# Units 2 and 3 move to the split convolution, with new instruction orders for the first eight tiles

## The chip, the core and the metric

The kernel runs on one core of one Trainium2 chip. The metric is the device time of one execution in microseconds (us): the median of three runs before the change is 705.1 us, with 704.99 and 705.26 as the lowest and the highest. The profile is of a fourth execution of its own; it took 705.18 us, of which the profiler's span, from the first to the last instruction that it shows, is 703.5 us. The remaining 1.7 us lie around the span.

## What is computed

A causal convolution of seven taps over the sequence, with one softmax-normalised set of taps for each of eight heads, followed by a two-layer feed-forward block whose activation is h·cos(h):

```python
def _attn_ref(x, weight):                 # x: 8 x 4096 x 192, weight: 8 x 7
    w = weight - np.max(weight, axis=-1, keepdims=True)
    w = np.exp(w)
    w = w / (np.sum(w, axis=-1, keepdims=True) + 1e-09)
    x_pad = np.concatenate([np.zeros((B, pad, D), dtype=np.float32), x], axis=1)
    idx = np.arange(S)[:, None] + np.arange(K)[None, :]
    x_unf = x_pad[:, idx, :].reshape(B, S, K, H, group)
    return np.einsum('hk,bskhg->bshg', w, x_unf).reshape(B, S, D)

def _moe_ref(x, w_in, w_out):             # 32768 tokens, 192 -> 2048 -> 192
    h = x @ w_in
    g = h * np.cos(h)
    return (g @ w_out).astype(np.float32)
```

## The kernel before

**Units and tiles.** The 32768 tokens are cut into 32 *units* of 1024 tokens. A unit is convolved and turned (transposed) so that the channels lie on partitions; then its two *tiles* of 512 tokens run through the feed-forward block. There are 64 tiles, called t0 to t63 below.

**A tile.** `mm1` (line 503) makes one of eight pairs of rows of `h` in PSUM with six matmuls; it is written `h0` to `h7` in the orders. `gcu` (lines 510 and 514) makes the cosine on ScalarE (ACT) and the product `g` on VectorE (DVE); this is `s0` to `s7`. `mm2_step` (line 552) is one step of the second product, two matmuls that sit in the two halves of the array's rows; `m13` is thirteen steps. A tile has 64 steps, and the steps of a tile lag its `h` by most of a tile. `h` has three PSUM buffers (`h_pool`, line 73), each of two banks, which the convolution of the next units also takes. The two output banks are copied out by `P` (ACT) and `Q` (DVE), line 571, and stored by `O`, line 574.

**Two ways to convolve.** Units 0 to 3 (`FIRST_RAW = 4`) are *whole*: `cast_unit` (`K`, line 219, GpSimd, here POOL) makes bf16; `conv_part` (line 229) runs four matmuls of 216 columns over all 128 rows for each of two halves of the heads, `d` and `c`; ACT copies them out (`ed`, `ec`, line 239); `double_unit` (`D`, line 307, POOL) doubles the result; `turn_unit` (`X`, line 326) turns 27 blocks by one DMA transpose; `mend_edges` (`Y`, line 394, POOL) repairs the first tokens of each block. Units 4 on are *split*: of a unit's nine blocks, five of 112 tokens go to TensorE in `conv_unit` (`c1`, `c2`, line 277: two groups of eight matmuls that use the two halves of the rows), ACT copies them out (line 294), and two transposes of 15 blocks turn them (`X` and `x`, line 317). The other 464 tokens are turned first (`T`, `turn_raw`, line 345), three taps are multiplied on ACT (`a`, line 356, six instructions a unit), the other four taps and all sums run on POOL (`R`, `conv_raw`, lines 363 to 377), and four DMAs put the result in place (`U`, `spread_raw`, line 387).

**What sets the order.** There is no scheduler: the program is recorded as it is written out in `PE_ORDER`, `ACT_ORDER`, `PE_FIRST` and `ACT_FIRST`, one string for each tile, and each engine runs its own instructions in that order. A letter in a PE string stands for matmuls (`h`, `m`, `c`, `d`, `r`, `w`) or for work of POOL or of SyncE (SP) that is recorded at that place: `K+3` in tile t is the cast of unit t//2+3, `L` its load, `T+3` its raw turn. `PE_FIRST` and `ACT_FIRST` hold the tiles with orders of their own, of which the last two of PE already resemble the later ones.

**The turn.** Where matmuls of the two row halves change places on one bank, `Turn` puts a no-operation on SP: it waits for the last matmul before the change (`mark`), and the first matmul after it waits for the no-operation (`wait`). That happens once a tile (between steps 31 and 32, lines 555 to 559) and once in each `conv_unit` (between `c1` and `c2`, lines 285 and 290). SP is also the queue from which nearly all loads, turns and stores are issued, in the order in which they were recorded. So TensorE can go on past these two points only when SP has got through everything recorded before.

```python
        turn = Turn()
        turn.mark(*ms)          # SP waits for the end of c1
        yield
        for h in range(4):
            ms = mm(h + 4, 0), mm(h, 1)
            if h == 0:
                turn.wait(*ms)  # c2 waits for SP
```

Of the kernel before, what the change touches and what calls it, by code (L numbers as in the profile page):

```python
# [16 lines left out]
def kernel(  # L17
# [8 lines left out]
    nc = tc.nc  # L26
    B, S, D = x.shape
    H, K = weight.shape
# [3 lines left out]
    T = 512  # L32
    NT = NTOK // T
    NB = T // 128
    U = 1024
    NU = NTOK // U
    UB = U // 128
    UPS = S // U
    TPU = U // T
    NF = Dff // 128  # L40
    NP = NF // 2
    NC = D // 64
    R = G // NC

    FIRST_RAW = 4
    NPB, OP = 5, 112
    NRB = 4
    OR = (U - NPB * OP) // NRB  # L50
# [1 line left out]
    PA = 3  # L52
# [120 lines left out]
    ct_bufs = [consts.tile([128, 2 * NC * NPB + 1, 64], BF16, name="ct_buf%d" % i) for i in range(2)]  # L173
# [166 lines left out]
    rT, pa, ro = {}, {}, {}  # L340
# [11 lines left out]
    def taps(u, j, half, mul):  # L352
        if u not in pa:
            pa[u] = pa_pool.tile([128, PA, WN, OR], FP32, name="pa")
        part = slice(HALF * half, HALF * (half + 1))
        mul(pa[u][:, j, part], tap_window(u, j)[:, part], tap[:, j : j + 1])  # L356

# [1 line left out]

    def conv_raw(u):  # L360

        a, p = pa.pop(u), raw_prod
        nc.gpsimd.tensor_tensor(out=p, in0=tap_window(u, PA, K),  # L363
                                in1=tap[:, PA:K].rearrange("p (j a b) -> p j a b", a=1, b=1).to_broadcast([128, K - PA, WN, OR]),
                                op=ALU.mult)
        add = nc.gpsimd.tensor_tensor
        n, done = K - PA, 0
        while done < PA:
            m = min(n, PA - done)
            add(out=p[:, 0:m], in0=p[:, 0:m], in1=a[:, done : done + m], op=ALU.add)  # L370
            done += m
        while n > 2:
            m = n // 2
            add(out=p[:, 0:m], in0=p[:, 0:m], in1=p[:, n - m : n], op=ALU.add)  # L374
            n -= m
        ro[u] = ro_pool.tile([128, WN, OR], BF16, name="ro")
        add(out=ro[u], in0=p[:, 0], in1=p[:, 1], op=ALU.add)  # L377
# [35 lines left out]
    for i, k in enumerate("DPDPDPDPDPDPDPAA"):  # L413
        q, rows = divmod(i, 4)
        three[k](out=band[32 * rows : 32 * rows + 32, HQ * q : HQ * (q + 1), 32 * rows : 32 * rows + E],  # L415
                     in_=diag[32 * q : 32 * q + 32])
    cast_unit(0, NB, UB)
    nc.gpsimd.memset(pick, 0.0)
    for i in range(2):
# [157 lines left out]
    def finish(t):  # L577
        o_sb[t] = opool.tile([128, NB, D], FP32, name="o_sb")
        for si in range(2):
            for b in range(2):  # L580
                copies[b](o_sb[t][:, 2 * b + si, :], o_ps.pop((t, b, si)))
                store(t, 2 * b + si, 2 * b + si + 1, [nc.scalar, nc.sync][b])
# [3 lines left out]

    PE_ORDER = ['m12 h0 m4 h1 K+3 R+1 m5 h2 m7 q h3 U+0 m6 h4 m17 h5 X+1 m9 p h6 h7 O m4', 'm11 h0 m4 h1 m6 h2 m7 q x+1 h3 m5 h4 m7 c1 m8 c2 m3 h5 T+3 L+4 m9 p O h6 h7 m4']
    ACT_ORDER = ['s0 s1 a211 s2 s3 s4 a014 a114 Q s5 P s6 s7 a007', 's0 s1 s2 a102 s3 a203 s4 Q ec2 ec1 s5 P s6 s7']  # L590

    PE_FIRST = ["K1 h0a h0b W0 h1 h2 h3 r h4 w5 d11 w4 h5 d21 W1 c11 X0 m1 h6 m11 h7 L2 c21 D1",
                "m6 K2 h0 m1 L3 h1 K3 m13 q h2 m3 h3 m9 h4 m6 h5 m3 X1 c12 m11 p c22 h6 d12 h7 L4 L5 m17 c13 m4 c23 m1 d22 Y1 D2 m1",
                "h0 m2 h1 m7 q K4 h2 m11 h3 X2 O m8 h4 Y2 m13 p h5 h6 m9 h7 m7",
                "h0 m8 h1 m8 q h2 m7 h3 m7 O m1 h4 m3 d13 m4 d23 m6 h5 m4 p T4 h6 h7 m4 D3 Z0 Z1",
                'm12 h0 m4 h1 K+3 m5 h2 m7 q h3 m6 h4 m17 h5 X+1 m9 p h6 h7 O m4',
                'm11 h0 m4 h1 m6 h2 m7 q x+1 Y3 h3 m5 h4 m7 c1 m8 c2 m3 h5 T+3 L+4 m9 p O h6 h7 m4']
    ACT_FIRST = ["s0a s0b s1 s2 er s3 s4 ed11 ed21 s5 ec11 s6 ec21 s7",
                "s0 s1 s2 s3 s4 s5 ec12 ec22 Q P s6 ed12 s7 ed22 ec13 ec23",
                "s0 s1 s2 s3 Q s4 P s5 s6 s7",  # L600
                "s0 s1 s2 s3 s4 ed13 ed23 Q s5 P s6 s7"] + ACT_ORDER

    PE_LAST = "m10 h0 m3 h1 m13 h2 m2 q h3 m10 h4 m3 h5 m7 h6 m12 p h7 O m7"
    ACT_LAST = "s0 s1 s2 s3 s4 s5 s6 P A s7"

    HALVES = {"": (0, NB), "a": (0, NB // 2), "b": (NB // 2, NB), "l": (0, NB // 2), "r": (NB // 2, NB)}
    conv = {"r": conv_rest()}
    for v in (1, 2, 3):
        for i, part in enumerate("dc"):
            conv[part, v] = conv_part(v, i, ring_banks)  # L610
    step, made, stored, done = 0, -1, 0, set()
    for t in range(NT + 1):
        u, second = divmod(t, TPU)
        cu = u + TPU
        if t >= 2 * TPU:
            if second:
                conv["c"] = conv_unit(cu, ring_banks) if cu < NU else iter(())
        pe = PE_LAST if t == NT - 1 else "m%d p" % (2 * STEPS * NT - step) if t == NT else PE_ORDER[second] if t >= len(PE_FIRST) else PE_FIRST[t]
        act = ACT_LAST if t == NT - 1 else ACT_ORDER[second] if t >= len(ACT_FIRST) else ACT_FIRST[t]
        act, h = act.split(), {}  # L620
        done = {k for k in done if k[0] in "cd" and k[2:]}

        def part_of(k):
            return k if k in conv else (k[0], int(k[2])) if k[2:] else k[0]

        def flush():
            while act:
                k = act[0]
                if k[0] == "e":
                    need = k[1:] if k[1:] in conv else k[1] + "2" + k[3:]  # L630
                else:
                    need = "p" if k in "PQA" else "h" + k[3:] if k[0] in "ab" else "h" + (k[1:2] if k[2:] in "lr" else k[1:])
                if need not in done:
                    return
                act.pop(0)
                if k in "PQA":
                    if 0 <= made < NT - 1:
                        evac(made, int(k != "P"), nc.scalar.copy if k == "A" else None)
                elif k[0] in "ab":
                    if u + 2 in rT:  # L640
                        taps(u + 2, int(k[1]), int(k[2]), nc.scalar.mul if k[0] == "a" else nc.vector.tensor_scalar_mul)
                elif k[0] == "e":
                    next(conv[part_of(k[1:])], None)
                elif k[0] == "s" and t < NT:
                    gcu(t, int(k[1]), h[k[1:2] if k[2:] in "lr" else k[1:]], *HALVES[k[2:]])

        def of_unit(k, v):
            if (k, v) == ("K", 1):
                cast_unit(1, 0, NB)
                cast_unit(1, NB)  # L650
            elif k == "Z":
                nc.gpsimd.memset(ct_bufs[v][0:OP], 0.0)
            elif (k, v) == ("X", 0):
                turn_unit(0, NB, UB)
            elif k == "L":
                load_unit(v)
                if v < FIRST_RAW:
                    load_edges(v)
            else:
                {"K": cast_unit, "D": double_unit, "X": turn_unit, "Y": mend_edges, "T": turn_raw, "R": conv_raw,  # L660
                 "U": spread_raw, "x": lambda u: turn_unit(u, part=1)}[k](v)

        for k in pe.split():
            if k[0] == "h":
                if t < NT:
                    h[k[1:]] = mm1(t, int(k[1]), *HALVES[k[2:]])
            elif k[0] in "rdc":
                next(conv[part_of(k)], None)
            elif k[0] == "m":
                for q in range(step, step + int(k[1:])):  # L670
                    mm2_step(q)
                step += int(k[1:])
            elif k[0] == "w":
                keep_warm(int(k[1:]), o_pools[0].tile([128, T], FP32, name="o_ps0"))
            elif k == "p":
                assert step % (2 * STEPS) == 0
                made = step // (2 * STEPS) - 1
            elif k == "q":
                assert step % (2 * STEPS) == STEPS
            elif k[0] == "W":  # L680
                cast_wo(int(k[1]))
            elif k == "O":
                while stored <= made and (stored, 0) in evacs and (stored, 1) in evacs:
                    store(stored)
                    stored += 1
            elif k[1:] and k[1] != "+":
                of_unit(k[0], int(k[1]))
            else:
                if u + int(k[2:]) < NU and (k[0] not in "RUx" or u + int(k[2:]) >= FIRST_RAW):
                    of_unit(k[0], u + int(k[2:]))  # L690
            done.add(k)
            flush()
            if k == "p" and made == NT - 1:
                finish(NT - 1)
        assert t == NT or not act


# [28 lines left out]
```

## Time and profile before

| | |
|---|---|
| median of three runs | 705.1 us |
| profiled execution | 705.18 us, span 703.5 us |
| TensorE (PE), busy | 697.0 us of the span |
| DVE, ACT, POOL, busy | 642.4, 644.4 and 503.7 us |
| granted TensorE clock, mean | 0.999 |
| one pair of tiles later on (from `h0` of t6 at 77.73 us to `h0` of t8 at 99.07 us) | 21.34 us |

The profile is a page of views of one execution. Its timeline names, for each engine, when a run of equal instructions began, how long it took, and what it waited for; the line number is that of the kernel before. "SPq" is the queue of SP: its duration is the time in which SP issues a transfer and can do nothing else, not the time until the data has landed. A mean duration of a matmul contains its latency, and its successors begin earlier: what matmuls cost on a full TensorE is read from the starts of the groups.

### The profile page before, as it was taken

What the parts mean: (1) busy time and instruction counts of PE and PEld (TensorE: products, weight loads), DVE (VectorE), ACT (ScalarE), POOL (GpSimd) and SP (SyncE); (2) the same over time, 40 slices, a digit from 0 to 9 for tenths busy, and PEclk for the clock granted to TensorE, in tenths of its full rate; (3) what the DMA queues carried; (4) which work ended last, traced back from release to release, by engine and by line L of the source; (5) the groups of instructions that cost most, each with busy time, mean ns of one, the idle gap of its engine ahead of it and who ended that gap; (6) DMA issues with size and microseconds to landing.
All of it is one profiled execution on the core that took longest, in us unless ns stands there. A gap on an engine that the chain in (4) does not pass through costs nothing.

```text
span 703.5 us, 26826 instructions
## 1 busy us (share of the span) xinstructions
PE 697.0 (99%) x11830; PEld 512.8 (73%) x11830; DVE 642.4 (91%) x598; ACT 644.4 (92%) x831; POOL 503.7 (72%) x214
## 2 busy tenths in 40 slices
PE   8999999999999999999999999999999999999997
PEld 4677777777777777777777777777777777777776
DVE  6889999999999999999999999999999999999996
ACT  7889999999999999999999999999999999999875
POOL 6524478977778877778877688877789778799400
PEclk9999999999999999999999999999999999999999
DMA  8964456667667768676656577577665576874331
GB/s 214 234 167 97 120 135 143 138 147 164 138 153 146 131 145 176 134 152 131 147 152 153 150 159 129 140 161 150 143 147 132 145 174 137 153 127 95 92 91 47
DMA packets 228292, 100.09 MB, mean 142 GB/s; under 512 B 156240, under 2 KB 227792, under 8 KB 228176
## 3 DMA queue, kind: packets, MB, share of 16 engines
q1 hardware_dynamic: 227464, 97.40, 62.7%
q8 instruction: 92, 1.51, 0.9%
q0 software_dynamic: 416, 0.79, 0.7%
q14 instruction: 24, 0.20, 0.1%
q10 hardware_dynamic: 296, 0.20, 0.1%
HBM read 31.36 MB, written 25.17 MB: 80 GB/s over the span
## 4 chain that ended last, share of the span: by engine, by line
PE 96%; DMA 1%; DVE 1%; POOL 0%; SPq 0%; ACT 0%; issue 0%; POOLq 0%
PE o_ps L552 48%; PE h L503 46%; PE h L277 2%; DMA wo_f<-in_moe_w_out_dram 1%; PE h L552 0%; SPq L124 0%; PE h L229 0%; DVE band L415 0%; POOL wo L120 0%; POOL mask L159 0%; DVE ct L438 0%; PE o_ps L432 0%; ACT mask L164 0%; DVE diag L404 0%; DVE prod L401 0%
## 5 line engine op out<-in xcount | busy, mean ns | idle before, releaser
L514 DVE TENSOR_TENSOR g<-h,cs 128x1024 bf16<-128x1024 f32 (+1 forms) x513 | 604.9, 1216 | 27.9 <-ACT cs L510 24.5
L510 ACT ACTIVATE cs<-h 128x1024 bf16<-128x1024 f32 (+1 forms) x513 | 511.0, 1021 | 44.0 <-PE h L503 30.6
L552 PEld LDWEIGHTS <-g 64*128 64x128 bf16 x8192 | 354.2, 94 | 102.2 <-issue 1.0
L552 PE MATMUL o_ps<-wo,g 64*128 64x192 bf16 x8128 | 420.6, 243 | 0.1
L503 PE MATMUL h<-cT,w 64*128 64x512 bf16 (+1 forms) x3078 | 407.0, 376 | 0.8 <-DVE g L514 0.4
L503 PEld LDWEIGHTS <-w 64*128 64x128 bf16 x3078 | 147.6, 94 | 75.0 <-issue 1.8
L211 POOL CAST xk<-x_f 128x768 bf16<-128x768 f32 (+1 forms) x56 | 76.4, 1367 | 113.9 <-DMA x_f<-in_x_dram 109.3
L363 POOL TENSOR_TENSOR raw_prod<-rT,tap 128x2784 f32<-128x2784 bf16 x28 | 135.3, 4832 | 0.2
L370 POOL TENSOR_TENSOR raw_prod<-raw_prod,pa 128x2088 f32<-128x2088 f32 x28 | 129.1, 4609 | 2.2
L356 ACT ACTIVATE pa<-rT,tap 128x348 f32<-128x348 bf16 x168 | 94.6, 580 | 0.0
L374 POOL TENSOR_TENSOR raw_prod<-raw_prod 128x1392 f32<-128x1392 f32 x28 | 87.9, 3138 | 2.2
L571 DVE COPY o_sb<-o_ps 128x384 f32<-128x384 f32 x62 | 34.6, 557 | 23.7 <-PE o_ps L552 23.5
L377 POOL TENSOR_TENSOR ro<-raw_prod 128x696 bf16<-128x696 f32 x28 | 46.5, 1660 | 2.2
L294 ACT CAST ct_buf<-h 112x480 bf16<-112x480 f32 x56 | 28.6, 562 | 4.1 <-PE h L277 0.6
L571 ACT COPY o_sb<-o_ps 128x384 f32<-128x384 f32 x64 | 30.8, 482 | 0.1
L277 PE MATMUL h<-xk,band 64*112 64x120 bf16 x448 | 21.2, 213 | 0.0
L277 PEld LDWEIGHTS <-band 64*112 64x112 bf16 x448 | 18.0, 127 | 0.0
L219 POOL CAST x_bf<-x_f 128x768 bf16<-128x768 f32 (+2 forms) x5 | 9.1, 1812 | 7.0 <-DMA x_f<-in_x_dram 6.9
L307 POOL COPY ct<-ct 128x1728 bf16<-128x1728 bf16 x3 | 4.9, 1630 | 8.9 <-ACT ct L239 8.9
L394 POOL COPY cT<-cT 128x144 bf16<-128x144 bf16 x3 | 0.9, 308 | 13.5 <-DMA cT<-ct 13.5
L136 PE MATMUL o_ps<-zero 128*128 128x512 bf16 x21 | 7.2, 492 | 1.3 <-DVE zero L131 1.3
L239 ACT CAST ct<-h 128x432 bf16<-128x432 f32 x12 | 5.9, 530 | 0.4 <-issue 0.4
(66 smaller groups left out, 52.7 us busy)
## 6 DMA issues: line engine op xcount, KB each, us to landing
out_dram<-o_sb SPq DMA_DIRECT2D x63, 384.0 KB, 3.7
x_f<-in_x_dram SPq DMA_DIRECT2D x28, 480.0 KB, 5.5
x_f<-in_x_dram SPq DMA_DIRECT2D x56, 192.0 KB, 2.7
cT<-ro SPq DMA_DIRECT2D x112, 87.0 KB, 2.3
x_f<-in_x_dram SPq DMA_DIRECT2D x4, 384.0 KB, 5.6
wo_f<-in_moe_w_out_dram SPq DMA_DIRECT2D x4, 384.0 KB, 7.9
x_f<-in_x_dram SPq DMA_DIRECT2D x2, 768.0 KB, 5.2
cT<-ct_buf SPq DMA_TRANSPOSE x56, 4.0
```

The lines of the kernel that those rows point to most:

```text
L211: copy(out=xk[u][:, NC * n0 : NC * n1].rearrange("p (k n) m -> p k n m", k=NC), in_=x_tiles[u][:, n0:n1].rearrange("p n (m k) -> p k n m", ...
L277: return nc.tensor.matmul(out=ps[h // 4][0:OP, 0 : NPB * 4 * G].rearrange("p (m i r) -> p i m r", m=NC * NPB, i=4)[:, h % 4], lhsT=band[si ...
L356: mul(pa[u][:, j, part], tap_window(u, j)[:, part], tap[:, j : j + 1])
L363: nc.gpsimd.tensor_tensor(out=p, in0=tap_window(u, PA, K), in1=tap[:, PA:K].rearrange("p (j a b) -> p j a b", a=1, b=1).to_broadcast([128, ...
L370: add(out=p[:, 0:m], in0=p[:, 0:m], in1=a[:, done : done + m], op=ALU.add)
L374: add(out=p[:, 0:m], in0=p[:, 0:m], in1=p[:, n - m : n], op=ALU.add)
L377: add(out=ro[u], in0=p[:, 0], in1=p[:, 1], op=ALU.add)
L503: nc.tensor.matmul(out=h[:, i, n0 * 128 : n1 * 128], lhsT=w[rows, k, j, :], rhs=rhs, start=(k == 0), stop=(k == NC - 1))
L510: nc.scalar.activation(out=cs[:, :, part], in_=h[:, :, part], func=AF.Sin, bias=math.pi / 2.0, scale=1.0)
L514: nc.vector.tensor_tensor(out=g_tiles[t][:, 2 * j : 2 * j + 2, part], in0=h[:, :, part], in1=cs[:, :, part], op=ALU.mult)
L552: ms.append(nc.tensor.matmul(out=o_ps[tt, b, si], lhsT=g_tiles[tt][rows, f, s * 128 : (s + 1) * 128], rhs=wo[rows, f // 2, f % 2, :], star ...
L571: (copy or copies[b])(o_sb[t][:, 2 * b : 2 * b + 2, :].rearrange("p s d -> p (s d)"), o_ps.pop((t, b)))
```

## The change

`FIRST_RAW` becomes 2: units 2 and 3 are split too. Their whole path goes (`d12 c12 d13 c13` and their copies, `D2 D3`, `Y2 Y3`, the two DMA transposes of 27 blocks, `load_edges`), and `c1 c2`, `T`, `R`, `U`, `x` and the taps come in. The two buffers `ct_buf` are no longer cleared whole between tiles (`Z0 Z1`, t3); only their unused columns are, at the start, on POOL ahead of the cast of unit 0's second half. Eight tiles instead of six have an order of their own; in t0 the casts and the matmuls keep their order, but three steps and four steps move ahead of `c11` and `h6`, and `c21` is recorded earlier. An `a` may now name its unit in a fourth digit. The marks `p` and `q` go: `m` counts the steps itself.

```diff
-    FIRST_RAW = 4
+    FIRST_RAW = 2
...
+    for buf in ct_bufs:
+        nc.gpsimd.memset(buf[0:OP, 0], 0.0)
+        nc.gpsimd.memset(buf[0:OP, 1:].rearrange("p (k n) m -> p k n m", k=NC)[:, :, NPB:], 0.0)
     cast_unit(0, NB, UB)
...
-    PE_FIRST = ["K1 h0a h0b W0 h1 h2 h3 r h4 w5 d11 w4 h5 d21 W1 c11 X0 m1 h6 m11 h7 L2 c21 D1",
-                "m6 K2 h0 m1 L3 h1 K3 m13 q h2 m3 h3 m9 h4 m6 h5 m3 X1 c12 m11 p c22 h6 d12 h7 L4 L5 m17 c13 m4 c23 m1 d22 Y1 D2 m1",
-                "h0 m2 h1 m7 q K4 h2 m11 h3 X2 O m8 h4 Y2 m13 p h5 h6 m9 h7 m7",
-                "h0 m8 h1 m8 q h2 m7 h3 m7 O m1 h4 m3 d13 m4 d23 m6 h5 m4 p T4 h6 h7 m4 D3 Z0 Z1",
-                'm12 h0 m4 h1 K+3 m5 h2 m7 q h3 m6 h4 m17 h5 X+1 m9 p h6 h7 O m4',
-                'm11 h0 m4 h1 m6 h2 m7 q x+1 Y3 h3 m5 h4 m7 c1 m8 c2 m3 h5 T+3 L+4 m9 p O h6 h7 m4']
-    ACT_FIRST = ["s0a s0b s1 s2 er s3 s4 ed11 ed21 s5 ec11 s6 ec21 s7",
-                "s0 s1 s2 s3 s4 s5 ec12 ec22 Q P s6 ed12 s7 ed22 ec13 ec23",
-                "s0 s1 s2 s3 Q s4 P s5 s6 s7",
-                "s0 s1 s2 s3 s4 ed13 ed23 Q s5 P s6 s7"] + ACT_ORDER
+    PE_FIRST = ["K1 h0a h0b h1 h2 W0 h3 r h4 W1 w5 d21 d11 w4 h5 m3 c11 m4 h6 c21 m4 X0 h7 m1 D1",
+                "L2 m7 h0 h1 L3 m13 h2 m3 h3 m6 K2 h4 T2 m6 X1 h5 K+3 m17 c1 c2 Y1 h6 m12 h7 m11",
+                "h0 O h1 m9 h2 m2 L4 m13 h3 m7 h4 X2 m10 h5 h6 m9 h7 m7",
+                "K4 h0 R2 x2 T3 m12 h1 m4 h2 m7 h3 m1 h4 m7 L5 c1 O m11 c2 m3 h5 m3 h6 h7 m4",
+                "m13 K+3 h0 h1 m12 T4 h2 m7 h3 m6 h4 O U+0 m17 X+1 h5 m5 h6 x+1 L+4 h7 m4",
+                "m10 h0 m4 h1 m6 h2 m8 O h3 m3 R3 m6 h4 m7 c1 m8 c2 h5 m8 h6 h7 m4",
+                "T+2 m15 h0 U+0 m4 h1 m8 h2 R+1 m9 h3 h4 m18 X+1 h5 m6 x+1 O h6 h7 m4",
+                "m11 h0 m4 h1 m6 h2 K+3 m7 h3 m3 h4 m11 L+4 c1 T+3 m6 c2 h5 m12 h6 O h7 m4"]
+    ACT_FIRST = ["ed11 s0a s0b s1 s2 er s3 s4 ed21 s5 ec21 ec11 s6 s7",
+                "s0 s1 s2 s3 s4 Q s5 P a0052 s6 ec1 ec2 s7 a0172",
+                "s0 a2002 s1 s2 a1122 s3 Q a2132 s4 P s5 s6 a1062 s7",
+                "s0 s1 s2 a102 s3 s4 ec2 ec1 Q s5 P s6 s7 a007",
+                "s0 s1 a1113 s2 a2123 s3 a0133 s4 Q a014 s5 P s6 s7 a2073",
+                "s0 a110 s1 s2 s3 a103 a003 s4 ec1 Q ec2 s5 P s6 a206 s7",
+                "s0 a2104 s1 a211 s2 s3 s4 a114 Q s5 P s6 s7 a007",
+                "s0 s1 a101 s2 s3 a203 s4 Q ec2 ec1 s5 P s6 s7 a017"]
...
-    for v in (1, 2, 3):
+    for v in (1,):
...
-        if t >= 2 * TPU:
-            if second:
-                conv["c"] = conv_unit(cu, ring_banks) if cu < NU else iter(())
+        if second:
+            conv["c"] = conv_unit(cu, ring_banks) if cu < NU else iter(())
...
-                    if u + 2 in rT:
-                        taps(u + 2, int(k[1]), int(k[2]), nc.scalar.mul if k[0] == "a" else nc.vector.tensor_scalar_mul)
+                    v = int(k[4]) if k[4:] else u + 2
+                    if v < NU:
+                        taps(v, int(k[1]), int(k[2]), nc.scalar.mul if k[0] == "a" else nc.vector.tensor_scalar_mul)
...
-            elif k == "Z":
-                nc.gpsimd.memset(ct_bufs[v][0:OP], 0.0)
...
             elif k[0] == "m":
-                for q in range(step, step + int(k[1:])):
-                    mm2_step(q)
-                step += int(k[1:])
+                for _ in range(int(k[1:])):
+                    mm2_step(step)
+                    step += 1
+                    if step % (2 * STEPS) == 0:
+                        made = step // (2 * STEPS) - 1
+                        done.add("p")
+                        flush()
+                        if made == NT - 1:
+                            finish(NT - 1)
```

From t8 on, and in the last tile, the orders differ from before only in that the marks `p` and `q` are gone.

On SP the first transfers after the second output weights are, before: `X0`, the loads of units 2 and 3, the turn of t0 (steps 31 and 32), `X1`, the loads of units 4 and 5, the turn of t1, `X2`. After: `X0`, the loads of units 2 and 3 (three DMAs each), the turn of t0, `T2`, `X1`, the turn of unit 2's `conv_unit`, the store of t0, the turn of t1, the load of unit 4, `X2` and `x2`, `T3`, the turn of t2, the load of unit 5, the turn of unit 3's `conv_unit`, the store of t1, `T4`, the turn of t3, the store of t2, `U2`, `X3`, `x3`, the load of unit 6, the turn of t4. On POOL the order after is: the casts of units 1, `wo`, `D1`, `K2`, `K3`, `Y1`, `K4`, `R2`, `K5`, `R3`, `R4`, `K6`, `K7`, `R5`.

## The prediction

> **What bounds the kernel now.** First the page's busy shares and its chain of waits:
>
> ```profile
> PE 697.0 (99%) x11830; PEld 512.8 (73%) x11830; DVE 642.4 (91%) x598; ACT 644.4 (92%) x831; POOL 503.7 (72%) x214
> ...
> PE 96%; DMA 1%; DVE 1%; POOL 0%; SPq 0%; ACT 0%; issue 0%; POOLq 0%
> ```
>
> The chain lies on TensorE from end to end; what counts is the time between the starts of its groups. The change touches t0 to t7, so I read the timeline of PE there, then of later tiles:
>
> ```profile
> 24.18 1.25 PE L552 MATMUL o_ps<-wo,g 64*128 64x192 bf16 x26
> 25.26 0.83 PE L503 MATMUL h<-cT,w 64*128 64x512 bf16 x6
> 25.90 0.43 PE L552 MATMUL o_ps<-wo,g 64*128 64x192 bf16 x6
> ...
> 29.33 0.43 PE L552 MATMUL o_ps<-wo,g 64*128 64x192 bf16 x6
> 29.69 0.54 PE L229 MATMUL h<-x_bf,band 128*128 128x216 bf16 x4
> 30.17 1.08 PE L552 MATMUL o_ps<-wo,g 64*128 64x192 bf16 x22
> ...
> 35.44 0.81 PE L503 MATMUL h<-cT,w 64*128 64x512 bf16 x6
> ...
> 72.40 0.39 PE L277 MATMUL h<-xk,band 64*112 64x120 bf16 x8
> 72.61 0.84 PE L552 MATMUL o_ps<-wo,g 64*128 64x192 bf16 x16
> ```
>
> From 24.18 on PE is dense: 26 matmuls (13 steps) fill 1.08 us, so a step costs 0.083; an `h` 0.65 (25.26 to 25.90); a group of the split convolution 0.21 (72.40 to 72.61). A group of the whole one costs more than its 0.48: m3 from 29.33 is over at 29.58, the next step begins at 30.17, so 0.59. The row at 35.44 is `h0` of t2.
>
> Third, SP and POOL, which feed these tiles:
>
> ```profile
> 25.62 5.15 SPq L326 DMA_TRANSPOSE cT<-ct  x1
> 30.93 3.08 SPq L98 DMA_DIRECT2D x_f<-in_x_dram  x6
> ...
> 60.00 4.05 SPq L326 DMA_TRANSPOSE cT<-ct  x1
> ...
> 72.94 1.21 SPq L345 DMA_TRANSPOSE rT<-xk  x1
> 74.21 1.61 SPq L98 DMA_DIRECT2D x_f<-in_x_dram  x3
> ```
>
> ```profile
> 22.53 1.63 POOL L307 COPY ct<-ct 128x1728 bf16<-128x1728 bf16 x1
> 25.87 2.56 POOL L219 CAST x_bf<-x_f 128x1728 bf16<-128x1728 f32 x1 [1.70 <-DMA x_f<-in_x_dram]
> ...
> 32.97 0.31 POOL L394 COPY cT<-cT 128x144 bf16<-128x144 bf16 x1 [0.41 <-DMA cT<-ct]
> ```
>
> `X1` cannot issue before 25.62, since SP first waits for step 31 of t0, the end of that m13. Its issue holds SP for 5.15 us; `X3`, with little else moving, needs 4.05. The data are there at 32.97, 7.35 after the start.
>
> **Part 1, TensorE's work.** Out go four groups of line 229 (c12, c13, d12, d13). By the starts around them, as above, they cost 0.59, 0.57, 0.58 and 0.57: 2.31 us. In come four groups of line 277 at 0.21: 0.84. Net **-1.47 us**; three of the four and two of the new lie ahead of `h0` of t2 (-1.32), the rest in t3 (-0.15). Steps and `h` stay the same in number.
>
> **Part 2, t0 up to 24.18: nothing.** `m` still waits for the cast of the second half of wo (21.12 to 22.6), which neither its load nor POOL's queue ahead of it moves. On ACT both copies of c21 now stand ahead of `s6`, some 0.5 us later; DVE was idle 0.63 us before the next product. The buffers' memsets: two of 1984 elements took 3.44 us (line 652), two of 64+960 should take 1.8. They sit on POOL after 8.13, where it was idle 3.59 us for a load until 11.73. Without that cover the cast behind them, and `r` at 13.92, would be up to 1.8 late.
>
> **Part 3, the hand-over at c2: a new wait.** c2 waits for a no-operation on SP, and in t1 this lies behind `T2` and `X1`. PE reaches the end of c1 at 24.18 + 45 steps (3.72) + four `h` (2.59) + 0.21 = 30.70. SP: `T2` at 25.62 at the earliest, after step 31 of t0 and after the first cast of `K2`. That cast follows `D1` (to 24.16) by 1.23 us, so 25.4, if its two small loads have landed; they are 384 of the 768 KB that before were complete by 25.87. Then `T2` and `X1` must issue. Undisturbed rows are 1.21 and 4.05. The longest rows are 2.33 (`T` at 115.63) and 5.15 (`X1` itself, here, with unit 3's load in flight): 1.1 more in either case. I count 1.1 once, since one backlog is to be waited out: 6.4 with the gaps, so SP is free at 32.05 and c2 starts at 32.2. **Wait 1.5 us.** Lower end: no surplus, c2 at 31.1, 0.4. Upper: both surpluses and the first cast 1 us late (landing 5.2 us after issue, as the whole unit did), c2 at 34.2, 3.5. Behind c2 stand h6, h7 and 23 steps, 3.41 us, so `h0` of t2 starts at 35.6, against 35.44. The other way to it: `X1` starts between 26.9 and 28.0, lands 7.35 later, `Y1` takes 0.31: 34.7 to 35.8, no later than c2 makes it. ACT's `s6`, the two copies of c2 and `s7` are queued behind h6, and DVE's last products behind them.
>
> The Trainium skill, "DMA: Bandwidth & Descriptors", section on why a DMA increments its semaphore by 16, lists for earlier generations 262,144 sequencer cycles to issue an SBUF-to-SBUF transpose of 8,192 tiles, so an issue grows with the tiles. With tiles of 16x128, and at the 1.2 GHz that the Trainium skill's "Trainium Kernel Development and Optimization", section NeuronCore Architecture, gives for SyncE, that is an estimated 1.28 us for `T2` (row: 1.21) and 5.76 for `X1` (rows: 4.05, 5.15); but for the 105 tiles of line 317 it is 2.8, and the row is 1.49. By that page of the Trainium skill c2 would wait 2.2 us; I stay with the rows.
>
> **Part 4, DVE and ACT in t2 to t6.** A tile asks DVE for eight products at 1.20 and a copy of 0.5: 10.1 us. PE needs 9.9 for t2 (57 steps, eight `h`) and 9.9 for t3 (52, eight, c1, c2). Before, t3 had 0.15 more and DVE had idled 1.8 us ahead of t2. Now `s7` of t1 stands behind c2's copies (35.05 to 36.05), and its product ends at 37.3; so DVE starts t2 without reserve, and `h0` and `h4` of t3 will find their buffers 0.1 to 0.2 late. ACT has four taps in t2 and five in t4: 8 x 0.92 + 5 x 0.48 + 0.47 = 10.2 of PE's 10.5. I add **+0.3**, between 0 (three buffers of `h` take it) and +0.8 (0.1 to 0.2 in each of five tiles).
>
> **Part 5, POOL's new chain: hidden, 0.** Step 95 at 37.7 releases `L4`; casts end some 8.6 later, as in 74.21 to 82.46 plus unit 4's memset, so 46.4. `R2` takes 14.47 (82.46 to 96.93), to 60.8. `U2` issues 2.7 and lands 2.2 later, 65.7; t5 asks for it at 66.7. `K5` 2.75 and `R3` end at 78.0. `U3` has issued by 80.8, and behind it on SP is the turn of t5, for which PE comes to step 352 (265 steps, 35 `h`, four groups after `h0` of t2) at 81.3. Cover 0.5 us. Each us by which POOL is later beyond that is a us of PE. By t8 POOL has R5 as early as before. `D`, `Y`, `Z` and their waits go, at no gain: POOL was not on the path.
>
> **Sum.** -1.47 + 1.5 + 0.3 = +0.3 on 705.18 us (span 703.5 and 1.7 around it), 705.5. The median lies 0.08 under the profiled run: **705.4 us**.
>
> **Rivals.**
> 1. *SP is through in time.* The undisturbed issues (5.3 us in all) let c2 go at 31.1, and `T2`'s data follow loads that were half done. If also `Y1` finds its data after 6.4 us, the lowest row of line 326, nothing is left of the wait: 705.1 - 1.47 = 703.6. With `Y1` at 34.7: 704.4. Against it: `X1`'s own row at this very place is 5.15. Chance 0.25, half of it below 703.7.
> 2. *Slower: SP is far behind at c2.* Place: c2 of t1; price: the upper end of part 3, 3.5 us for 1.5; 705.4 + 2.0 less the slack that DVE then regains, 707.2. It decides from a wait of about 2.6 us. For it: the DMA share was 1.16 in this stretch; against: the cast needs half of the unit only. Chance 0.17, in which 0.02 is for a clock that falls: the granted clock is 1.00 in every stretch before the end, but PE never waits over 1.3 us there; should a wait of 3.5 bring half clock for as long again, that is 1.7 more, 708.9. The Trainium skill, "TensorE: Matmul & The Clock Gate", Part 1, has such a rule: an idle window of about 3.4 us halves the clock. No stretch of this trace tests it.
> 3. *POOL's chain is late in t6.* `L4` shares the queues with `X2`, `x2` and a store; 1.5 us late makes PE wait 1.0 at step 352: 706.4. Chance 0.10, half of it above 706.5.
>
> That the change is not what it says is out: the built program has 16 matmuls of line 277 for each of the two units.
>
> **Numbers.** My forecast has 0.48, its own range 704.7 to 706.3 (part 3 by +-0.7, part 4 by its ends). 0.2% is 1.4 us, about what a measurement of this kernel can tell from no change. Below 703.7: half of rival 1, 0.13. Above 706.5: rival 2 and half of rival 3, 0.22. Between: 0.65. The range 703.8 to 707.2 leaves out the best of rival 1 and the worst of rival 2.
>
> **What would show it.** In PE's timeline of t1, c1 near 30.5 and c2 near 32.2, with SP's row of `X1` ending just before c2. `h0` of t2 at 35.6; t5's `h0` 0.2 to 0.4 later than the 66.77 of before; 21.34 a pair from t6 on. POOL's `R2` from 46 to 61 and no wait at step 352. I am wrong if c2 follows c1 at once, if `h0` of t2 waits for `Y1` long after c2, or if PE waits in t5 or t6.

## The result and the profile after

The changed kernel takes 706.65 us (median of 11 runs, 706.24 to 708.02), the kernel before 705.1 us beside it (11 runs, 704.98 to 705.62): ratio 1.0025, 95% interval 1.0017 to 1.0033. So it is slower, by 0.17 to 0.33%; the bound of 0.2% lies inside that interval. The profiled execution is the shortest of the eleven, 706.24 us with a span of 704.5, 1.0 more than before. In the profile this 1.0 us can be followed: 0.76 of it stands at `h0` of t8, 0.82 at the last matmul, and the rest lies behind that. The 0.4 us from the profiled execution to the median cannot be followed; the last experiments come back to it.

The page after, busy shares and chain of waits:

```profile
PE 697.4 (99%) x11846; PEld 513.2 (73%) x11846; DVE 642.7 (91%) x598; ACT 647.3 (92%) x839; POOL 527.0 (75%) x222
...
PE 97%; DVE 1%; ACT 1%; POOL 0%; issue 0%; SPq 0%; POOLq 0%
```

The chain is still on TensorE, and PE's timeline shows where it waits (start, duration, engine, line, operation, tiles, count, and in brackets a wait):

```profile
24.00 1.25 PE L558 MATMUL o_ps<-wo,g 64*128 64x192 bf16 x26
...
30.32 0.39 PE L277 MATMUL h<-xk,band 64*112 64x120 bf16 x8
31.52 0.42 PE L277 MATMUL h<-xk,band 64*112 64x120 bf16 x8 [0.82 <-SPq L196]
...
34.97 1.46 PE L509 MATMUL h<-cT,w 64*128 64x512 bf16 x12
...
49.52 0.26 PE L558 MATMUL o_ps<-wo,g 64*128 64x192 bf16 x2
49.87 0.82 PE L509 MATMUL h<-cT,w 64*128 64x512 bf16 x6
50.52 0.76 PE L558 MATMUL o_ps<-wo,g 64*128 64x192 bf16 x14
...
59.47 1.03 PE L558 MATMUL o_ps<-wo,g 64*128 64x192 bf16 x14
60.33 0.81 PE L509 MATMUL h<-cT,w 64*128 64x512 bf16 x6
...
81.31 1.19 PE L558 MATMUL o_ps<-wo,g 64*128 64x192 bf16 x18
...
99.83 0.83 PE L509 MATMUL h<-cT,w 64*128 64x512 bf16 x6
```

c1 starts at 30.32 and c2 at 31.52; a group lasts 0.21, so c2 waited 0.99. The row at 34.97 is `h0` and `h1` of t2, 0.47 earlier than before. Then small waits give it back. The single step at 49.52 needs 0.08 and `h4` of t3 starts 0.35 later: 0.27 waited. The row of 14 matmuls at 59.47 needs 0.86 until the next row, one like it at 50.52 (up to line 277 at 51.09) needs 0.57: 0.29 are waited inside the row. In the row at 81.31 it is 0.28. `h0` of t8 (99.83) stands 0.76 later than before (99.07).

What follows is read from this timeline in the same way for every kernel: a matmul of a step fills 0.041 us, one of `h` 0.108, one of line 277 0.026, and what lies between two starts beyond that is a wait. From 24 us to t8 the changed kernel waits 0.99 at c2 and 1.5 in ten further places behind it, 1.26 of it between 46 and 95 us. The kernel before has none there but the 0.1 at each change to line 229, which the prediction counted in that line's 0.58.

SP and POOL after:

```profile
25.43 1.21 SPq L345 DMA_TRANSPOSE rT<-xk  x1
26.74 4.67 SPq L326 DMA_TRANSPOSE cT<-ct  x1
...
45.19 1.68 SPq L345 DMA_TRANSPOSE rT<-xk  x1
...
77.81 3.43 SPq L389 DMA_DIRECT2D cT<-ro  x4
```

```profile
33.38 0.31 POOL L396 COPY cT<-cT 128x144 bf16<-128x144 bf16 x1 [3.45 <-DMA cT<-ct]
...
45.93 4.82 POOL L365 TENSOR_TENSOR raw_prod<-rT,tap 128x2784 f32<-128x2784 bf16 x1
```

`X1` leaves SP at 31.41, the no-operation of c1 goes through behind it, c2 starts at 31.52. `Y1` finds its data at 33.38, 6.64 after `X1` began; `R2` begins at 45.93; `U3` (77.81) has issued by 81.24.

### The profile page after: what moved, and what is told of

It is laid out like the page before. It is cut to its first block, busy times and chain, and to the rows that moved or that the text cites. A ratio compares the mean times of both kernels' runs of the same rounds, so it can differ in the third digit from the quotient of the medians.

```text
span 704.5 us, 26896 instructions
## 1 busy us (share of the span) xinstructions
PE 697.4 (99%) x11846; PEld 513.2 (73%) x11846; DVE 642.7 (91%) x598; ACT 647.3 (92%) x839; POOL 527.0 (75%) x222
## 4 chain that ended last, share of the span: by engine, by line
PE 97%; DVE 1%; ACT 1%; POOL 0%; issue 0%; SPq 0%; POOLq 0%
PE o_ps L558 47%; PE h L509 47%; PE h L277 2%; DVE g L520 1%; ACT cs L516 1%; PE h L558 0%; DVE band L417 0%; ACT ct L478 0%; POOL mask L159 0%; ACT mask L164 0%; ACT ct L444 0%; DVE diag L406 0%; DVE cT L463 0%; PE o_ps L438 0%; PE h L459 0%
## 5 line engine op out<-in xcount | busy, mean ns | idle before, releaser
L211 POOL CAST xk<-x_f 128x768 bf16<-128x768 f32 (+1 forms) x60 | 81.9, 1368 | 115.7 <-DMA x_f<-in_x_dram 99.9
L365 POOL TENSOR_TENSOR raw_prod<-rT,tap 128x2784 f32<-128x2784 bf16 x30 | 144.9, 4828 | 0.2
L372 POOL TENSOR_TENSOR raw_prod<-raw_prod,pa 128x2088 f32<-128x2088 f32 x30 | 138.3, 4610 | 2.7 <-ACT pa L357 0.4
L357 ACT ACTIVATE pa<-rT,tap 128x348 f32<-128x348 bf16 x180 | 101.9, 581 | 0.0
L376 POOL TENSOR_TENSOR raw_prod<-raw_prod 128x1392 f32<-128x1392 f32 x30 | 94.1, 3137 | 2.3
L379 POOL TENSOR_TENSOR ro<-raw_prod 128x696 bf16<-128x696 f32 x30 | 49.7, 1658 | 2.4
L294 ACT CAST ct_buf<-h 112x480 bf16<-112x480 f32 x60 | 30.6, 562 | 5.1 <-PE h L277 1.6
L136 PEld LDWEIGHTS <-zero 128*128 128x128 bf16 x24 | 2.4, 116 | 4.6 <-issue 2.7
L219 POOL CAST x_bf<-x_f 128x768 bf16<-128x768 f32 (+1 forms) x3 | 3.9, 1310 | 1.8 <-DMA x_f<-in_x_dram 1.7
L120 POOL CAST wo<-wo_f 128x1536 bf16<-128x1536 f32 x2 | 2.9, 1470 | 2.3 <-DMA wo_f<-in_moe_w_out_dram 2.3
```

What stands on the lines that cost most here:

```text
L211: copy(out=xk[u][:, NC * n0 : NC * n1].rearrange("p (k n) m -> p k n m", k=NC), in_=x_tiles[u][:, n0:n1].rearrange("p n (m k) -> p k n m", ...
L365: nc.gpsimd.tensor_tensor(out=p, in0=tap_window(u, PA, K), in1=tap[:, PA:K].rearrange("p (j a b) -> p j a b", a=1, b=1).to_broadcast([128, ...
```

## The experiments

Theory A held the wait at c2 for the cause, passed through to the end one for one; theory B held that ACT and DVE set the pace of t2 to t6, whatever c2 does. Theories S, D, C, W and V were formed on the way. The table gives every kernel that settles something, with the kernel before beside it on the same chip (705.10 to 705.14). "Waits" are those of PE from 24 us to `h0` of t8 in the profiled execution; "stretch" is the time from m13 of t1 to `h0` of t8 less the 74.89 of the kernel before. The last two columns come from one profiled execution each. The intervals of neighbouring rows overlap, so a difference of some tenths of a us between two medians is not shown by the medians alone; what the text says of such a difference rests on the places of the waits in the timeline.

| kernel | median (range, runs) | ratio, 95% interval | waits | stretch |
|---|---|---|---|---|
| changed kernel, again | 706.64 (706.04 to 709.30, 7) | 1.0026 [1.0015, 1.0037] | 2.47 | +0.92 |
| c2 later | 707.51 (707.01 to 708.37, 5) | 1.0035 [1.0023, 1.0047] | 3.24 | +1.70 |
| unit 2's taps on POOL | 706.87 (706.47 to 709.46, 9) | 1.0029 [1.0020, 1.0039] | 2.83 | +1.26 |
| SP busier at c2 | 708.59 (708.13 to 709.88, 5) | 1.0053 [1.0041, 1.0065] | 4.40 | +2.88 |
| X1 first | 706.21 (705.84 to 706.96, 11) | 1.0015 [1.0007, 1.0024] | 1.99 | +0.48 |
| respaced | 706.30 (705.65 to 709.65, 11) | 1.0024 [1.0015, 1.0033] | 1.92 | +0.47 |
| X1 first, respaced, taps on POOL | 704.77 (704.31 to 706.56, 11) | 1.0000 [0.9991, 1.0008] | 0.66 | -0.87 |
| the same, steps moved | 705.67 (704.74 to 708.14, 12) | 1.0013 [1.0003, 1.0023] | 2.42 | +0.89 |

In each row the stretch is the waits less the 1.47 us that part 1 of the prediction had worked out, to within 0.1. So the saving is there in every kernel, and only the waits decide. In part this agreement is bookkeeping, since a wait is what is left of a stretch when the matmuls' fixed times are taken off; what it does show is that these times hold in all the kernels. The saving by itself is seen with three edits, where the stretch is shorter than before.

### Four runs on the hand-over at c2

**The changed kernel again.**

> The changed kernel once more, as the base for the others on the same chip. Both theories: 706.3 to 707.0 us, 1.2 to 1.9 over the kernel before. In its profile c2 of t1 starts 0.8 to 1.5 us after the end of c1, and the small waits of PE from t2 to t6 add up to 1.2 to 1.6 us.

It gave the same waits as the first profile, to 0.01 each, though t1 began 0.2 later. So the waits belong to the order, and not to one execution.

**c2 later.** One string is changed, so that 1.64 us of other work stand between c1 and c2:

```diff
-"... m17 c1 c2 Y1 h6 m12 h7 m11"
+"... m17 c1 h6 m12 c2 Y1 h7 m11"
```

> c2 of t1 moved behind h6 and twelve steps, so that PE has 1.64 us of other work while SP issues X1; nothing else changes. Theory A (the wait at c2 goes through to the end one for one): the 0.99 us between c1 and c2 goes, h0 of t2 starts near 34.0 instead of 34.97, and the time falls by 0.8 to 1.1 us, to 705.5 to 705.9. Theory B (ACT and DVE set the pace from t2 to t6, whatever c2 does): h0 of t2 is as early, but the waits of t2 to t6 grow by as much, and the time falls by less than 0.4 us.

```profile
30.20 0.39 PE L277 MATMUL h<-xk,band 64*112 64x120 bf16 x8
...
32.05 0.39 PE L277 MATMUL h<-xk,band 64*112 64x120 bf16 x8
...
35.74 1.47 PE L509 MATMUL h<-cT,w 64*128 64x512 bf16 x12 [1.75 <-POOL cT L396]
```

```profile
35.38 0.31 POOL L396 COPY cT<-cT 128x144 bf16<-128x144 bf16 x1 [5.23 <-DMA cT<-ct]
```

The wait at c2 is gone, and a longer one of 1.92 stands at `h0` of t2, which now waits for `Y1`. `X1` had begun at 26.63, so its data took 8.75 us here against 6.64. Both theories missed this: a second limit stands right behind the first. With 6.64 us `Y1` would have been through in time; why the landing took 2.1 longer here no run shows, but the shortest of the five runs (707.01) speaks against a single bad execution. The waits between 46 and 95 us are the same 1.26.

**Unit 2's taps on POOL.** The six multiplications of `taps` for unit 2 go from ACT to POOL.

> The six taps of unit 2 are multiplied on POOL (idle from 33.7 to 40.7) instead of on ACT; same values, same orders. Theory B (ACT is too full in t1 and t2): six times 0.48 us less on ACT, the waits of PE from t2 to t4 shrink from 1.0 to under 0.5 us, and the time falls by 0.5 to 0.9 us. Theory A: the wait at c2 stays at 0.8 to 1.0 us, and the time falls by less than 0.2 us.

The waits between 46 and 95 us are 1.27, place by place as before. ACT's load with unit 2's taps is not their cause, and theory B falls in that form. c2 waited 1.32, more than the 0.8 to 1.0 expected, because SP issued `X1` for 4.99 us in this execution in place of 4.67.

**SP busier at c2.** The load of unit 4 (`L4`, three transfers) is recorded behind `X1`, ahead of c1's no-operation, in place of its own in t2.

> The load of unit 4 is recorded behind X1 in t1 instead of in t2, so that SP issues three more DMAs (1.4 us, as in its row now) ahead of the no-operation that c2 waits for. Theory A: c2 waits 1.4 us more, 2.2 to 2.5 in all, and the time rises by 1.2 to 1.5 us, to 707.9 to 708.2. Theory B: c2 waits as long, but ACT and DVE catch up meanwhile, the waits of t2 to t6 shrink, and the time rises by 0.2 to 0.8 us.

c1 starts at 30.32 as in the changed kernel, and c2:

```profile
33.47 0.42 PE L277 MATMUL h<-xk,band 64*112 64x120 bf16 x8 [2.76 <-SPq L196]
```

c2 waits 2.94 in place of 0.99, and the median grows by the same 1.95: 708.59 against 706.64. The wait at c2 does pass through one for one. Its size was expected 0.5 smaller: the three transfers took 1.49 us as said, but `X1` took 0.27 longer and the gap behind it came on top.

### Three runs on X1 and on the orders

**A respacing that failed.** Tiles 3, 4 and 6 get the distances between `h` that the later tiles have.

> Tiles 3, 4 and 6 keep their steps in number and their loads, casts and transposes, but the tiles' h groups stand as far apart as in the later tiles (m4 between h0 and h1, m5 or m6 ahead of h4). c2 of tile 1 is left as it is. Theory S (the small waits of tiles 3 to 7 come from h groups that stand too close for the chain h, cosine, product, free buffer): the waits of TensorE from 46 to 95 us, 1.27 us together in the changed kernel, fall to 0.3 or less, the wait at c2 stays near 1.0, the first product of tile 8 comes at 98.9 in place of 99.83, and the time is 705.5 to 705.9. Theory D (VectorE and ScalarE have more to do in tiles 2 and 3 than TensorE, whose tiles there have 57 and 55 steps in place of 64, so that the same time must be waited somewhere): waits of 0.8 or more stay in tiles 3 to 5, wherever the groups stand, and the time is 706.3 to 706.8.

It took 793.34 us (793.05 to 796.75; ratio 1.1262 [1.1243, 1.1281]). My new t3 had 55 steps, the old one 52, so the number was not kept. The page's row of the second product, and the end of t3 in the timeline:

```profile
L558 PE MATMUL o_ps<-wo,g 64*128 64x192 bf16 x8128 | 443.1, 243 | 66.5 <-ACT o_sb L577 60.7
```

```profile
53.05 0.49 PE L558 MATMUL o_ps<-wo,g 64*128 64x192 bf16 x8
54.73 0.42 PE L558 MATMUL o_ps<-wo,g 64*128 64x192 bf16 x6 [1.18 <-ACT o_sb L577]
```

In the changed kernel a tile's output sums are complete just ahead of `h6`, and while DVE and ACT copy them out, PE makes `h6` and `h7` (1.3 us). Three steps earlier the border falls inside a run of steps: PE goes on to the next sums, whose banks are still being copied out, and waits 1.2 to 1.5 in each later tile. The turn in the middle of the sums, three steps early as well, costs 0.28 a tile more; 60 tiles by 1.45 make the 87 us over the changed kernel.

**X1 first.** `X1` is recorded in the place of `T2`, and `T2` behind c1's no-operation; h6 stands between c1 and c2; a tap of unit 2 moves into t2.

```diff
-"... K2 h4 T2 m6 X1 h5 K+3 m17 c1 c2 Y1 h6 m12 h7 m11"
+"... K2 h4 X1 m6 h5 K+3 m17 c1 T2 h6 c2 Y1 m12 h7 m11"
-"s0 s1 s2 s3 s4 Q s5 P a0052 s6 ec1 ec2 s7 a0172"
-"s0 a2002 s1 s2 a1122 s3 Q a2132 s4 P s5 s6 a1062 s7"
+"s0 s1 s2 s3 s4 Q s5 P s6 ec1 ec2 s7 a0172"
+"s0 a2002 s1 s2 a1122 s3 Q a2132 s4 P a0042 s5 s6 a1062 s7"
```

> In tile 1 the transposes of unit 1 (X1) are recorded in the place of T2, T2 behind c1's no-op, and h6 stands between c1 and c2; the first tap of unit 2 moves from tile 1 into tile 2. Theory A (two limits stand one behind the other: SP's queue ahead of c1's no-op, and the landing of X1 with Y1 behind it): X1 starts at 25.4 in place of 26.74, c1's no-op is free when c1 ends, no wait at c2 over 0.2; Y1 comes at 32.0 to 32.5 where the landing keeps its 6.6 us, and h0 of tile 2 at 34.0 to 34.2 in place of 34.97; the time is 705.6 to 705.9 and the spread of the runs is smaller. Where the landing takes 8.7 us as with c2 set back, Y1 comes at 34.2, h0 at 34.5 to 34.7 and the time is 706.1 to 706.4. Theory C (what is won at c2 is taken back by later waits, since the engines behind TensorE set the pace of tiles 2 to 6): h0 of tile 2 comes earlier, but the waits of tiles 3 to 7 grow from 1.3 to 2.2 and the time stays at 706.4 to 706.7.

```profile
30.39 0.39 PE L277 MATMUL h<-xk,band 64*112 64x120 bf16 x8
...
31.25 0.39 PE L277 MATMUL h<-xk,band 64*112 64x120 bf16 x8
...
34.01 1.47 PE L509 MATMUL h<-cT,w 64*128 64x512 bf16 x12
```

Neither c2 nor `h0` of t2 waits: `h0` stands at 34.01, 0.96 earlier, as theory A said. But from there to `h4` of t3 15.48 us pass in place of 14.90, 0.58 more. ACT shows why: its first tap of unit 2 waits 0.67 for `T2`, now issued 5.5 us later, and the cosines of t2 queue up behind it. The median falls by 0.43, not by 0.9. Theory C was right that some comes back, but what starts it is one late transpose.

**Both together** repeats the three extra steps, took 793.33 us (792.60 to 793.95) and tells nothing more.

> Both of the two edits before. If A and S hold and their gains add up, the two waits of 1.0 and 1.3 us are gone, TensorE keeps what four groups of L229 for four of L277 save (1.47), and the time is 704.2 to 704.8, below the kernel before (705.1). If C or D holds, what one edit wins is waited for elsewhere, and the time is no better than that of the better one of the two alone, 705.5 to 706.4.

### Three runs with the right number of steps

**Respaced.** Tile 1 as in the changed kernel; t3 has 52 steps again:

```diff
-"K4 h0 R2 x2 T3 m12 h1 m4 h2 m7 h3 m1 h4 m7 L5 c1 O m11 c2 m3 h5 m3 h6 h7 m4"
-"m13 K+3 h0 h1 m12 T4 h2 m7 h3 m6 h4 O U+0 m17 X+1 h5 m5 h6 x+1 L+4 h7 m4"
+"K4 h0 R2 x2 T3 m10 h1 m4 h2 m6 h3 m5 h4 m5 L5 c1 O m9 c2 m3 h5 m6 h6 h7 m4"
+"m12 K+3 h0 m4 h1 m5 T4 h2 m7 h3 m6 h4 O U+0 m17 X+1 h5 m9 h6 x+1 L+4 h7 m4"
...
-"T+2 m15 h0 U+0 m4 h1 m8 h2 R+1 m9 h3 h4 m18 X+1 h5 m6 x+1 O h6 h7 m4"
+"T+2 m12 h0 U+0 m4 h1 m5 h2 R+1 m7 h3 m6 h4 m17 X+1 h5 m9 x+1 O h6 h7 m4"
```

> The respacing of tiles 3, 4 and 6 once more, now with the 52 steps that tile 3 has in the changed kernel (the first try had 55, and so moved the border between two tiles' output sums by three steps for the rest of the kernel); tile 1 as in the changed kernel. Theory S (the small waits come from h groups that stand too close): the waits of TensorE from 46 to 95 us, 1.27 us together, fall to 0.3 or less, the first product of tile 8 comes at 98.8 to 99.0 in place of 99.83, and the time is 705.4 to 705.8. Theory D (tiles 2 and 3 hold less work for TensorE, 9.9 us each, than for VectorE, 10.2, so that the difference is waited wherever the groups stand): 0.6 us or more of waits stay, and the time is 706.0 to 706.6.

```profile
48.63 0.94 PE L558 MATMUL o_ps<-wo,g 64*128 64x192 bf16 x12
49.41 0.81 PE L509 MATMUL h<-cT,w 64*128 64x512 bf16 x6
...
59.38 0.74 PE L558 MATMUL o_ps<-wo,g 64*128 64x192 bf16 x14
59.96 0.81 PE L509 MATMUL h<-cT,w 64*128 64x512 bf16 x6
```

The waits from 46 to 95 us fall from 1.26 to 0.54, the median by 0.34; with c2's wait at 1.19 in this execution the stretch is +0.47. What remains led to a reason that none of the theories had. The row of 14 at 59.38 is dense now; a new wait of 0.28 stands in the row at 48.63, where the changed kernel has none. Count the steps. t3 begins at step 144, and the turn of tile 2 lies between steps 159 and 160, 16 steps in. The old t3 has `h2` at that place (m12, m4, `h2`); the new one has it inside m6. In the changed kernel the turns of t4 and t6 lie 28 steps in, inside m7 and inside m9, which are just the two rows with 0.28; the new orders have `h3` there and no wait. So 0.28 to 0.30 is what a hand-over through SP costs with SP free, wherever no other work stands in it; the later tiles of the respacing that failed show the same. Of the 1.26 this is 0.57. Of the rest, 0.27 ahead of `h4` of t3 and 0.15 and 0.14 around the start of t4 went with the distances, as theory S had it, while t6 has a new 0.13.

**X1 first, respaced, unit 2's taps on POOL.** All three edits above together.

> X1 ahead of T2 as before, the six taps of unit 2 on GpSimd in place of ScalarE, and the respaced tiles 3, 4 and 6. Theory S: no wait at c2, h0 of tile 2 at 34.0, and no more than 0.4 of small waits up to 95 us; the time is 704.2 to 704.8, under the kernel before by 0.3 to 0.9. Theory D: waits of 0.6 or more come up in tiles 2 and 3, as with X1 first alone, and the time is 705.0 to 705.6.

c2 and `h0` of t2 (34.26, with t1 0.3 later than in the changed kernel) do not wait, t2 has no wait over 0.06, t3 only the 0.28 of its turn. POOL waits 2.4 for `T2`, and nobody waits for POOL. 704.77 us is 1.9 below the changed kernel; against the kernel before the ratio is 1.0000 [0.9991, 1.0008], no difference that these runs can show, though its shortest run (704.31) is 0.6 below the shortest of before (704.94).

**The same, steps moved.** Six steps go from t1 into t2 and t3, three each, and t2 is respaced.

> As the run before, but six steps of TensorE move out of tile 1, three into tile 2 and three into tile 3, so that tiles 1, 2 and 3 hold some 11.3, 10.1 and 10.1 us of its work in place of 11.8, 9.9 and 9.9. Theory D: the waits that the run before still has in tiles 2 and 3 go, and the time is below it by 0.3 or more, at 704.2 to 704.6. Theory S: nothing is left to win there, and the time is that of the run before within 0.2. h0 of tile 2 would stand at 33.5, so Y1 (32.5 with X1 first) may be the next to be late: then 0.2 to 0.5 is waited there.

It was 0.9 slower. Of its waits, 0.29 and 0.28 are turns that the new t2 and t3 again put inside a run of steps, and 1.24 ahead of `h5` of t3 is the matter of the next runs. It gives theory D no support, but with these waits in it no clean answer either.

### Two runs on the spread

The kernel before spreads over 0.6 us, the changed one over 1.8 to 3.3. In both runs three steps of t1 move behind `h0` (m4 h0 m3 h1 for m7 h0 h1).

> The run with X1 first, unit 2's taps on GpSimd and tiles 3, 4 and 6 respaced (704.77, 704.31 to 706.56), with one thing more: three steps of tile 1 go behind h0, so that the first step that reads the second half of the output weights stands 0.65 later, and h1 has 0.25 longer for its buffer. Theory W (the wait of 0.25 to 0.56 at 22 us and the spread of the runs come from the varying landing of those weights, whose cast starts between 20.4 and 21.3): no wait over 0.1 before 24 us, the median at 704.1 to 704.4, the highest run within 1.0 of the lowest. Rival V (the spread comes from what lands later, the loads of units 2 and 3 or the transposes of unit 1): the median falls by 0.3 at most and the spread stays at 2 us.

> The same move alone in the changed kernel (706.64, 706.04 to 709.30). Theory W: no wait before 24 us, the median 706.1 to 706.4 and the spread within 1.0. Rival V: c2's wait for SP takes the place of what is won (X1 starts no earlier), the median stays within 0.2 of 706.6 and the spread at 2 us or more.

The first took 705.07 us (704.18 to 707.54, 11 runs; 1.0002 [0.9993, 1.0011]), the second 706.93 (706.27 to 708.76, 11 runs; 1.0027 [1.0018, 1.0036]). The spread stays, the wait of 0.25 before 24 us stays too (now ahead of `h1`), and theory W falls. But the profiled execution of the first was a long one, 706.68, and shows what one such execution did. ACT, SP and PE in t3:

```profile
46.16 2.00 ACT L516 ACTIVATE cs<-h 128x1024 bf16<-128x1024 f32 x2 [0.45 <-PE h L509]
50.37 0.59 ACT L357 ACTIVATE pa<-rT,tap 128x348 f32<-128x348 bf16 x1 [2.21 <-DMA rT<-xk]
```

```profile
37.78 7.48 SPq L317 DMA_TRANSPOSE cT<-ct_buf  x2
45.37 1.69 SPq L345 DMA_TRANSPOSE rT<-xk  x1
```

```profile
50.98 0.41 PE L558 MATMUL o_ps<-wo,g 64*128 64x192 bf16 x6
53.18 0.82 PE L509 MATMUL h<-cT,w 64*128 64x512 bf16 x6 [1.79 <-DVE g L520]
```

The first tap of unit 3 stands on ACT between `s2` and `s3`. It waits 2.21 us for `T3`, the cosines of `h3` and `h4` wait behind it, DVE behind ACT, and PE finds no free buffer for `h5`: 1.95 us. In the run with the steps moved (profiled at 706.04, its shortest 704.74) the same tap waits 1.59 and PE 1.24. In the kernel with the three edits, profiled at 704.70, it does not wait:

```profile
48.56 0.59 ACT L357 ACTIVATE pa<-rT,tap 128x348 f32<-128x348 bf16 x1
```

There `T3` had begun at 44.41, 0.96 earlier than in the long execution, in which SP was busy for 7.48 us with `X2` and `x2` ahead of it (6.13 here). Its data landed 3.3 us after it began, and the tap stands 4.15 behind the start: 0.85 were left. In the changed kernel the two are 4.24 apart (45.19 and 49.43), and the data landed after 3.2: 1.0 was left. In the two executions with a wait the data landed 4.8 to 5.0 after `T3` began, and ACT had come to the tap 3.2 and 2.8 after that start. So the reserve is about 1 us; a late start of `T3` and a landing 1.5 to 1.7 later together used it up, and what goes beyond shows on PE. Why the landing was later is open. That the longer runs of the changed kernel itself have this cause is not shown: none of them was profiled, and in its two profiled executions the landing took 3.1 and 3.2.

## Why the prediction was right or wrong

The forecast was 705.4 us, 0.3 above before and within 0.2% of it; measured is 706.65, 1.5 above. The range of 703.8 to 707.2 holds it, the forecast's own range (704.7 to 706.3) does not. The median lies just above 706.5, where the prediction put a chance of 0.22, and it came there in neither of the two ways from which that chance was made up (SP far behind at c2, POOL late in t6). The sign and the main mechanism were right, three sizes were not. With the measured terms the sum is -1.47 + 0.99 + 1.5 = 1.0, against 0.94 in the stretch and 1.0 in the span.

- **Part 1, -1.47: right.** A new group fills 0.21 where nothing is waited for (51.09 to 51.30), and all kernels of the table give the 1.47 back when their waits are added.
- **Part 2, nothing: right.** m13 of t1 began at 24.00, in other executions of the changed orders at 23.88 to 24.33; before it was 24.18.
- **Part 3, wait of 1.5 at c2: right in mechanism, 0.5 too long.** c1 was done at 30.53 (30.70 said) and c2 started at 31.52 (32.2). `X1`'s row ends just before c2, as said; but `T2` and `X1` showed only 0.6 of the 1.1 us of surplus that I counted, and SP took `T2` up at 25.43. Half a us less of surplus and 0.2 less ahead of `T2`, with c1 done 0.2 earlier, make the 0.5. By the turns seen later, some 0.28 would be waited there even with SP free, as the price of the hand-over itself; no run has c2 right behind c1 with SP free. I priced the way by `Y1` as no later than c2, which held (33.69), but not how close it stood: with c2 set back it became the bound.
- **Part 4, +0.3 for DVE and ACT: this is the step that failed.** 1.5 was waited. The `h4` of t3 was named, with 0.1 to 0.2 for 0.27. But the reason given, products and cosines for which PE leaves too little time, covers only a part; 0.57 are two turns that the new orders of t4 and t6 put inside a run of steps. In the strings before, the mark `q` stood at the turn, and an `h` behind every `q`. I read its removal as bookkeeping. That `h0` of t5 came at 67.03, 0.26 later than before and just as forecast, was luck: c2's wait was 0.5 too long in the sum and the waits of t2 to t4 were too short.
- **Part 5, POOL's chain hidden: right.** `R2` ran from 45.9 to 60.4, and `U3` had issued at 81.24, ahead of step 352. PE does wait 0.28 there, in t6, which the prediction had named as a sign of being wrong; but it is its turn, and with `h3` at that place it is gone.
- **The median.** I put it 0.08 below the profiled run. It lies 0.4 above. The taps queued on ACT 4.24 us behind their transpose were in no term of the sum; by the last runs they are a possible cause, not a shown one.

Rival 1 (no wait at c2, 703.6 to 704.4) comes near the kernel with the three edits, at 704.77. Rival 2 had the right place; its wait of over 2.6 us was met only when SP was loaded on purpose. There, with 2.94 us waited from 30.5 on, the granted clock was 1.00 from 30.0 to 33.5 and 1.00 again from 33.5 to 37.0. That agrees with the rule of the Trainium skill, "TensorE: Matmul & The Clock Gate", Part 1, that the clock falls after an idle window of about 3.4 us; no run here waited long enough to test it. Rival 3 did not occur.

For the issue of `X1` I stayed with the rows (4.05 and 5.15) against the 5.76 us estimated from the Trainium skill, "DMA: Bandwidth & Descriptors", section on why a DMA increments its semaphore by 16. It took 4.48 to 4.99 us in the traces, so the rows were the better guide; for `T2` both said 1.2 to 1.3, and it took 1.21.

## What to carry to other kernels

Where one engine is dense to the end, write the balance as the work saved less the waits that the new order makes, and read each wait from the starts of the groups: here that closes to 0.1 us in every kernel of the table, and it shows at once that the saving was not lost but waited away. When marks or asserts vanish from an order written by hand, count where its hand-overs now fall; each should have some other work in it, and a border moved by three steps cost 87 us. An instruction that waits for a transfer should not stand in the queue of an engine that is on the way to the bound: on POOL the same wait of 2.4 us cost nothing, on ACT 2.2 us cost PE 1.95.

## What the runs showed of the hardware

The transposes' time to land varies far more than their time to issue. Over the thirteen traces with the changed orders, `X1` took 4.48 to 4.99 us to issue and landed 6.0 to 7.0 us after its start, and once 8.7; `T3` took 1.2 to 1.8 to issue and landed after 2.8 to 5.0, against a median of 3.3 for all of its kind. A hand-over from PE through an idle SP and back took 0.28 to 0.30 in every place where no other work stood in it.
